# Linear attention into a two-layer MLP: the start of batch 0 reordered, batch 2 transposed by DMA, the last output tile in two column halves

## The chip, the cores and the metric

The kernel runs on one core of a Trainium2 chip. The metric is the device time of one execution in microseconds, over several runs of the same program; lower is better. Besides, one execution was recorded by the hardware profiler, and all rows below come from that one. Engines are named as in its page: PE multiplies matrices (PEld is its loading of the stationary operand), DVE and ACT are the vector and scalar engines, POOL is the general engine that here issues the loads, SP issues the stores and the other transfers.

## What is computed

```python
batch, n_heads, seq, head_dim = (8, 8, 576, 64)      # q, k, v, float32
n_tokens, d_model, d_ff = (4608, 512, 2048)          # w_in [512, 2048], w_out [2048, 512]

def phi(x):
    return np.where(x > 0, x, np.exp(x) - 1.0) + 1.0
q_p, k_p = (phi(q), phi(k))
kv = np.einsum('bhsd,bhse->bhde', k_p, v)
z = np.sum(k_p, axis=2)
num = np.einsum('bhsd,bhde->bhse', q_p, kv)
den = np.einsum('bhsd,bhd->bhs', q_p, z)[..., None] + 1e-06
attn = num / den
x = attn.transpose(0, 2, 1, 3).reshape(4608, 512)
h = x @ w_in
g = h - np.tanh(h)
out = g @ w_out
```

kv and z need k (kv needs v too), den needs q and z, and num needs q and kv. So 1/den can be had without v.

## The kernel before

**Tiling.** Attention goes by batch (eight of 576 tokens), the MLP by chunk (nine of 512 tokens). x is kept transposed in `xT`, 128 rows for each of four head pairs p. Layer 1 of a chunk is 16 tiles `fi` of 128 hidden columns, each of four matmuls with 512 moving columns over p (L270); ACT's tanh (L275) and DVE's subtraction (L276) turn each into a slice of `gT`. Layer 2 gives four output tiles `i` of 128 tokens, each of 16 matmuls with 512 columns (L285), then a copy by ACT (L290) and two stores by SP (L293).

**Attention of a batch.** `phi` (L120) is one exp on ACT, then two instructions on DVE, `r` and the product, for each half `i` of the heads; q and k each have two such halves. q is transposed into `qT`, either by PE with an identity matrix and copies from PSUM (`a_qT_pe`, L146: five tiles that ACT copies, four that DVE copies, for each half) or by one DMA of SP (`a_qT_dma`, L140). `kv_mm` (L161) makes kv with 18 matmuls for each half; a third block of ones behind v makes z in the same matmuls. `a_kv` or `a_kv_half` multiplies the result with a mask into `kz`. `a_den` (L185) makes den and its reciprocal `rden`. The reciprocal is then spread over the partitions: by two DMA steps through DRAM for batches from 2 on (`a_spread`, L205), by PE and a selection matrix `sel` for batches 0 and 1 (`a_spread_pe`, L252). num is made by `num_mm` (L217). For batches from 2 on DVE multiplies it with the spread reciprocal from PSUM straight into `xT` (`a_num`, L228); for batches 0 and 1 ACT first copies it to `ns` (L245) and DVE scales it later (`a_scale`, L262).

**Buffers.** PSUM is one tile of eight banks, handed out in a fixed order: in the chunks from 1 on, six for the MLP (`dense`) and two for attention (`attn`, banks 6 and 7). The raw k and q have one buffer each, v, `qT` and `kz` two.

**Order.** The order of the instructions on each engine is written out by hand and is the order of the program text; the framework adds only the waits. Before the loops, batch 0 goes through attention alone (L337 to L358): 36 matmuls on zeros keep PE busy, then come phi of k, phi of q, and the rest. POOL first issues the loads of k, q and v of batch 0, then makes the identity, then loads `w_in` (L300 to L305). In the loop over chunks, the work of attention of the next two batches is hung behind certain tiles: `s1[fi]` runs behind layer-1 tile `fi`, `s2[s]` behind a quarter (four matmuls) of an output tile of layer 2. Batch 1 runs in chunk 0, batch 2 from the end of chunk 0 into chunk 1. The only transposes by PE in the loops are those of batch 1 (chunk 0) and of batch 2 (chunk 1, L406, one part behind each of the tiles 4 to 7).

Of the kernel before, what the change touches and what calls it, by code (L numbers as in the profile page):

```python
# [18 lines left out]
def kernel(  # L19
# [74 lines left out]
    def load_k(b):  # L94
        load_kq(b, k, k_t, "kraw")

    def load_q(b):
        load_kq(b, q, q_t, "qraw")
# [32 lines left out]
    def a_kphi(b, i):  # L131
        phi(b, k_t, kp_t, "kp", i)

    def a_qphi(b, i):
        phi(b, q_t, qp_t, "qp", i)
# [10 lines left out]
    def a_qT_pe(b, i, banks, parts=(0, 1)):  # L146
        if i == 0 and 0 in parts:
            new_qT(b)
        for n in parts:
            j0, j1 = ((0, 5), (5, 9))[n]  # L150
            ps = banks().bitcast(BF16).rearrange("p (j t) -> p j t", t=128)
            for j in range(j0, j1):
                nc.tensor.transpose(ps[:, j - j0, :], qp_t[b][:, i, j].rearrange("p h d -> p (h d)"), ident)
            src = ps[:, 0:j1 - j0, :]
            dst = qT_t[b][:, i, j0:j1].rearrange("p j g t -> p j (g t)")
            if n == 0:
                nc.scalar.copy(dst, src)  # L157
            else:
                nc.vector.tensor_copy(dst, src)

    def kv_mm(b, i, ps):  # L161
        kp, vt = kp_t[b], v_b[b % 2]
        for j in range(J):
            for hg in range(2):
                r = slice(64 * hg, 64 * hg + 64)
                nc.tensor.matmul(ps[hg], kp[r, i, j].rearrange("p h d -> p (h d)"),  # L166
                                 vt[r, i, :, j, :], start=(j == 0), stop=(j == J - 1))
# [6 lines left out]
        for hg in range(2):  # L174
            nc.vector.tensor_mul(kz_t[b][:, hg], ps[hg][:, :, 0:160], mask[:, hg])  # L175

    def a_kv_half(b, i, banks):
        if i == 0:
            kz_t[b] = work.tile([128, 2, 2, 160], BF16, name="kz")
        ps = [banks()[:, 0:192] for hg in range(2)]  # L180
        kv_mm(b, i, ps)
        for hg in range(2):
            nc.vector.tensor_mul(kz_t[b][:, hg, i, :], ps[hg][:, 0:160], mask[:, hg, i, :])

    def a_den(b, banks):  # L185

# [58 lines left out]
    def a_num_copy(b, ns, p, banks):  # L245
        ps = num_mm(b, p, banks)
        if p < NP:
            nc.scalar.copy(ns[:, p, 0:8, :], ps)
        else:
            nc.scalar.copy(ns[:, :, 8, :], ps[:, 0:NP, :])  # L250

    def a_spread_pe(b, bank0, pairs):  # L252

        bp = ps_all[:, bank0:bank0 + 4, :]
        for n, p in enumerate(pairs):
            for t in range(4):
                r = slice(32 * t, 32 * t + 32)
                nc.tensor.matmul(bp[:, t, 144 * n:144 * n + 144], sel[r, p].rearrange("p h e -> p (h e)"),  # L258
                                 rden_t[b][r], start=True, stop=True)
        return bp  # L260

    def a_scale(b, p, ns, bp, o):  # L262
        nc.vector.tensor_mul(  # L263
            xT[:, p, S * b:S * b + S].rearrange("p (j t c) -> p t j c", j=J, t=4),
            ns[:, p].rearrange("p j (t c) -> p t j c", t=4),
            bp[:, :, o:o + 144].rearrange("p t (j c) -> p t j c", c=16))


    def l1mm(c, fi, h, p):
        nc.tensor.matmul(h, w_in_sb[:, p, fi * 128:(fi + 1) * 128], xT[:, p, c * 512:(c + 1) * 512],  # L270
                         start=(p == 0), stop=(p == NP - 1))

    def l1act(fi, h, gT):
        th = mpool.tile([128, 512], F32, name="th")
# [10 lines left out]
            nc.tensor.matmul(o, gT[:, fi, i * 128:(i + 1) * 128], w_out_sb[:, fi, :],  # L285
                             start=(fi == 0), stop=(fi == NF - 1))

    def evac(c, i, o):
        osb = opool.tile([128, DM], F32, name="osb")
        nc.scalar.copy(osb, o)  # L290
        for half in range(2):
            b, j = divmod(2 * (4 * c + i) + half, J)
            nc.sync.dma_start(out=out[b * S:(b + 1) * S, :].rearrange("(p j) m -> p j m", j=J)[:, j, :],  # L293
                              in_=osb[64 * half:64 * half + 64])


    nc.vector.memset(zero, 0.0)  # L297
    act0 = rpool.tile([128, 1], F32, name="act0")
    nc.scalar.activation(act0, zero[:, 0:1], AF.Exp)
    load_k(0)  # L300
    load_q(0)
    load_v(0)
    make_identity(nc, ident)
    for g in range(4):
# [29 lines left out]
        rest -= part  # L334


    for n in range(36):  # L337
        nc.tensor.matmul(ps_all[:, n % 4, :], zero[:, 0:128], zero, start=True, stop=True)  # L338
    for i in range(2):
        a_kphi(0, i)  # L340
    for i in range(2):
        a_qphi(0, i)
    side, kvb = Banks([4, 5, 6, 7]), Banks([0, 1, 2, 3])
    a_qT_pe(0, 0, side)
    a_kv_half(0, 0, kvb)
    a_qT_pe(0, 1, side)
    ns0 = new_ns(0)
    for p in (0, 2):
        a_num_copy(0, ns0, p, side)
    a_kv_half(0, 1, kvb)  # L350
    a_den(0, Banks([0]))
    a_num_copy(0, ns0, NP, Banks([1]))
    for p in (1, 3):
        a_num_copy(0, ns0, p, side)
    bp_a = a_spread_pe(0, 0, (0,))
    bp_b = a_spread_pe(0, 4, (1, 2, 3))
    for p in range(NP):
        a_scale(0, p, ns0, bp_b if p else bp_a, 144 * (p - 1) if p else 0)  # L358
    load_q(2)
    load_k(2)  # L360
    load_v(2)
# [1 line left out]
    for c in range(NC):  # L363
        gT = gpool.tile([128, NF, 512], BF16, name="gT")
        n1, n2 = c + 1, c + 2
        s1 = {i: [] for i in range(16)}
        s2 = {i: [] for i in range(16)}
        if c == 0:
            side = Banks([4, 5, 6, 7])
            sub = {}  # L370

            def spread1(h):
                sub["bp"] = a_spread_pe(1, 4, (2 * h, 2 * h + 1))
                for p in (2 * h, 2 * h + 1):
                    a_scale(1, p, sub["ns"], sub["bp"], 144 * (p % 2))

            s1[11].append(lambda: a_kphi(1, 0))
            s1[13].append(lambda: a_kphi(1, 1))
            s1[15].append(lambda: a_qphi(1, 0))
            s2[1].append(lambda: a_qphi(1, 1))  # L380
            s2[4].append(lambda: a_qT_pe(1, 0, side))
            s2[5].append(lambda: a_qT_pe(1, 1, side))
            s2[6].append(lambda: a_kv(1, side))
            s2[8].append(lambda: a_den(1, side))
            def num1():
                sub["ns"] = new_ns(1)
                for p in (NP, 0, 1, 2, 3):
                    a_num_copy(1, sub["ns"], p, side)
                load_v(3)

            s2[9].append(num1)
            s2[11].append(lambda: spread1(0))
            s2[13].append(lambda: spread1(1))
            s2[14].append(lambda: a_qphi(2, 0))
            s2[15].append(lambda: a_qphi(2, 1))
        elif n1 < B:
            s1[9 if c == 1 else 5].append(lambda: a_kv(n1, attn))
            s1[11 if c == 1 else 8].append(lambda: (a_den(n1, attn), a_spread(n1)))
            for p in range(NP + 1):
                s2[9 + p].append(lambda p=p: a_num(n1, p))  # L400
            if c + 3 < B:
                s1[10].append(lambda: load_v(c + 3))
        if c == 1:
            s1[1].append(lambda: a_kphi(2, 0))
            s1[3].append(lambda: (a_kphi(2, 1), load_k(3), load_q(3)))
            for n in range(4):  # L406
                s1[4 + n].append(lambda n=n: a_qT_pe(2, n // 2, attn, (n % 2,)))
        if c >= 1 and n2 < B:
            if c > 1:

                s1[0].append(lambda: (gate(gT, 0), load_k(n2), load_q(n2)))
            d = 4 if c == 1 else 2
            s2[d].append(lambda: a_kphi(n2, 0))
            s2[d + 2].append(lambda: a_kphi(n2, 1))
            s2[d + 4].append(lambda: a_qphi(n2, 0))
            s2[d + 6].append(lambda: (a_qphi(n2, 1), a_qT_dma(n2)))
        if c == 0:

            hs = [ps_all[:, fi, :] for fi in range(4)]
            first = Banks([4, 5, 6, 7, 0, 1, 2, 3])  # L420
            for p in range(NP):
                for fi in range(4):
                    l1mm(c, fi, hs[fi], p)
            for fi in range(4):
                l1act(fi, hs[fi], gT)
        for fi in range(4 if c == 0 else 0, NF):
            h = first() if c == 0 else dense()
            for p in range(NP):
                l1mm(c, fi, h, p)
            l1act(fi, h, gT)  # L430
            for f in s1[fi]:
                f()
        os_ = {}
        for s in range(16):

            (g, i) = divmod(s, 4) if c == 0 else (s % 4, s // 4)
            if g == 0:
                os_[i] = ps_all[:, i, :] if c == 0 else dense()
            l2mm(gT, os_[i], i, 4 * g, 4 * g + 4)
            if g == 3:  # L440
                evac(c, i, os_[i])
            for f in s2[s]:
                f()
# [30 lines left out]
```

## Time and profile before

| | |
|---|---|
| median of three runs | 302.88 us (302.36 to 304.21) |
| the profiled execution | 303.09 us |
| its span, first to last instruction | 301.3 us |
| mean granted PE clock | 0.998 of full |
| L270, layer 1 | 576 matmuls, 128.5 us |
| L285, layer 2 | 576 matmuls, 131.6 us |
| L166, kv | 288 matmuls, 13.7 us |
| DMA queues, share of 16 engines' span | loads by POOL 37.8%, those of SP 29.0% |

In the rows of the timeline the columns are: start in us from the start of the span; duration of the row; engine; line; operation; what is written and what is read; shape; count; and in brackets the idle time of the engine just before and what ended it. The busy time of a row with a count can hold idle time between its instructions. A stretch of the busy-time view shows, behind the length, each engine's busy us with its number of instructions, then the granted clock, the DMA share and GB/s.

Chunk 0 runs from 19.9 to 53.3 us in that execution, chunk 1 to 87.3, and the last matmul ends at 296.4. Each load of k or q of batch 0 is 144 KB, in four parts; the parts of one tensor are issued some 0.6 us apart.

### The profile page before, as it was taken

To read this page: it belongs to the slowest core of one execution; us is meant where nothing else is said; L and a number is where in the kernel's file an instruction comes from. 1 tells how busy PE (TensorE), PEld (TensorE's weight loads), DVE (VectorE), ACT (ScalarE), POOL (GpSimd) and SP (SyncE) were. 2 spreads that over 40 slices of the span, in tenths; PEclk is the share of its full clock that TensorE was granted. 3 is DMA by queue.
4 is the path that set the end of the run, shared out by engine and by line. 5 is a ranking of instruction groups with operands and counts; after the bars stand their busy time and mean duration, and the time that the engine had idled before them with its cause. 6 is when DMAs were issued, how large, how long until landed. Compare 5 with 4: busy or idle time off the path is not lost.

```text
span 301.3 us, 4706 instructions
## 1 busy us (share of the span) xinstructions
PE 291.9 (97%) x1790; PEld 138.3 (46%) x1790; DVE 180.2 (60%) x304; ACT 149.6 (50%) x230; POOL 52.1 (17%) x91
## 2 busy tenths in 40 slices
PE   8989999989999999999999999999999999999993
PEld 3454454444445444544454445444544444444441
DVE  7658944887557854785478557865681467008500
ACT  3638914954734653565256625662562166136420
POOL 8873263051006000600050003000000000000000
PEclk9999999999999999999999999999999999999999
DMA  6999999677969786967697778477108310130033
GB/s 90 189 207 206 205 207 205 181 120 135 212 111 177 122 200 138 155 116 190 140 151 135 179 148 128 87 173 148 38 4 193 71 35 0 37 86 18 2 70 70
DMA packets 36406, 38.23 MB, mean 127 GB/s; under 512 B 14432, under 2 KB 31008, under 8 KB 35616
## 3 DMA queue, kind: packets, MB, share of 16 engines
q0 software_dynamic: 17600, 18.35, 37.8%
q1 hardware_dynamic: 18784, 19.58, 29.0%
q8 instruction: 14, 0.23, 0.3%
q14 instruction: 8, 0.07, 0.1%
HBM read 43.78 MB, written 9.55 MB: 177 GB/s over the span
## 4 chain that ended last, share of the span: by engine, by line
PE 79%; DMA 9%; DVE 5%; ACT 2%; issue 1%; POOL 1%; SPq 0%; DVEq 0%; POOLq 0%; ACTq 0%
PE ps_all L270 38%; PE ps_all L285 33%; DMA qraw<-in_q_dram 4%; PE ps_all L166 4%; DMA out_dram<-osb 2%; DVE gT L276 2%; PE ps_all L221 2%; DMA v<-in_v_dram 2%; ACT e L127 1%; ACT osb L290 1%; DVE kp L129 1%; PE ps_all L191 1%; POOL kraw L85 1%; DVE r L128 1%; DVE qp L129 1%
## 5 line engine op out<-in xcount | busy, mean ns | idle before, releaser
L285 PE MATMUL ps_all<-w_out_sb,gT 128*128 128x512 bf16 x576 | 131.6, 379 | 0.0
L270 PE MATMUL ps_all<-xT,w_in_sb 128*128 128x512 bf16 x576 | 128.5, 379 | 0.2 <-DVE xT L263 0.2
L276 DVE TENSOR_TENSOR gT<-ps_all,th 128x512 bf16<-128x512 f32 x144 | 96.8, 687 | 53.0 <-ACT th L275 52.6
L275 ACT ACTIVATE th<-ps_all 128x512 f32<-128x512 f32 x144 | 85.3, 600 | 51.7 <-PE ps_all L270 47.2
L285 PEld LDWEIGHTS <-gT 128*128 128x128 bf16 x576 | 55.5, 98 | 65.7 <-issue 0.2
L270 PEld LDWEIGHTS <-w_in_sb 128*128 128x128 bf16 x576 | 55.2, 98 | 65.9 <-issue 1.1
L290 ACT COPY osb<-ps_all 128x512 f32<-128x512 f32 x36 | 21.1, 586 | 79.6 <-PE ps_all L285 59.5
L232 DVE TENSOR_TENSOR xT<-ps_all,rdb 128x512 bf16<-128x512 f32 x24 | 16.4, 689 | 11.8 <-PE ps_all L221 11.8
L104 POOL DMA_DIRECT2D v<-in_v_dram x32 | 19.2, 615 | 18.7 <-PE ps_all L166 5.7
L127 ACT ACTIVATE e<-kraw 128x1152 bf16<-128x1152 bf16 x16 | 18.5, 1165 | 5.1 <-DMA kraw<-in_k_dram 5.1
L129 DVE TENSOR_TENSOR kp<-e,r 128x1152 bf16<-128x1152 bf16 x16 | 12.1, 759 | 14.1 <-ACT e L127 13.0
L127 ACT ACTIVATE e<-qraw 128x1152 bf16<-128x1152 bf16 x16 | 18.4, 1166 | 0.9 <-DMA qraw<-in_q_dram 0.9
L129 DVE TENSOR_TENSOR qp<-e,r 128x1152 bf16<-128x1152 bf16 x16 | 12.1, 758 | 8.1 <-ACT e L127 7.3
L281 POOL COPY g<-gT 1x1 bf16<-1x1 bf16 x4 | 0.7, 176 | 92.9 <-DVE gT L276 92.9
L166 PE MATMUL ps_all<-v,kp 64*128 64x192 bf16 x288 | 13.7, 243 | 0.0
L166 PEld LDWEIGHTS <-kp 64*128 64x128 bf16 x288 | 11.5, 94 | 3.5 <-issue 2.9
L338 PE MATMUL ps_all<-zero 128*128 128x512 bf16 x36 | 10.4, 461 | 1.2 <-DVE zero L297 1.2
L221 PE MATMUL ps_all<-qT,kz 128*128 128x512 bf16 x32 | 11.3, 380 | 0.0
L89 POOL DMA_DIRECT2D kraw<-in_k_dram x14 | 8.7, 628 | 11.8 <-ACT qT L157 10.4
L89 POOL DMA_DIRECT2D qraw<-in_q_dram x14 | 8.7, 642 | 5.9 <-DVE r L128 5.9
L263 DVE TENSOR_TENSOR xT<-ns,ps_all 128x576 bf16<-128x576 f32 x8 | 5.6, 750 | 5.0 <-PE ps_all L258 5.0
L175 DVE TENSOR_TENSOR kz<-ps_all,mask 128x320 bf16<-128x320 f32 x14 | 6.2, 485 | 3.7 <-PE ps_all L166 3.7
(45 smaller groups left out, 92.8 us busy)
## 6 DMA issues: line engine op xcount, KB each, us to landing
out_dram<-osb SPq DMA_DIRECT2D x72, 128.0 KB
rdb<-ds SPq DMA_DIRECT2D x12, 576.0 KB
v<-in_v_dram POOLq DMA_DIRECT2D x32, 144.0 KB, 6.7
kraw<-in_k_dram POOLq DMA_DIRECT2D x14, 288.0 KB, 5.0
qraw<-in_q_dram POOLq DMA_DIRECT2D x14, 288.0 KB, 6.8
w_in_sb<-in_moe_w_in_dram POOLq DMA_DIRECT2D x4, 512.0 KB, 10.1
w_out_sb<-in_moe_w_out_dram POOLq DMA_DIRECT2D x4, 512.0 KB, 12.1
kraw<-in_k_dram POOLq DMA_DIRECT2D x4, 144.0 KB, 3.8
```

The lines of the kernel that those rows point to most:

```text
L89: nc.gpsimd.dma_start(out=t[64 * hg:64 * hg + 64].rearrange("p i h j d -> p (i h) (j d)"), in_=src[b, 4 * hg:4 * hg + 4].rearrange("h (p j ...
L104: nc.gpsimd.dma_start(out=v_b[b % 2][64 * hg:64 * hg + 64, i, 0:2].rearrange("p h j d -> p h (j d)"), in_=v[b, h0:h0 + 2].rearrange("h (p ...
L127: nc.scalar.activation(e, x, AF.Exp)
L129: nc.vector.tensor_tensor(store[b][:, i].rearrange("p j h d -> p h j d"), e, r, ALU.min)
L166: nc.tensor.matmul(ps[hg], kp[r, i, j].rearrange("p h d -> p (h d)"), vt[r, i, :, j, :], start=(j == 0), stop=(j == J - 1))
L221: nc.tensor.matmul(ps, kz[:, p // 2, p % 2, 0:128], qT[:, p % 2, 0:8, p // 2, :], start=True, stop=True)
L232: nc.vector.tensor_mul(xT[:, p, S * b:S * b + 512].rearrange("p (j t c) -> p j t c", j=8, t=4), ps.rearrange("p j (t c) -> p j t c", t=4), ...
L270: nc.tensor.matmul(h, w_in_sb[:, p, fi * 128:(fi + 1) * 128], xT[:, p, c * 512:(c + 1) * 512], start=(p == 0), stop=(p == NP - 1))
L275: nc.scalar.activation(th, h, AF.Tanh)
L276: nc.vector.tensor_sub(gT[:, fi, :], h, th)
L285: nc.tensor.matmul(o, gT[:, fi, i * 128:(i + 1) * 128], w_out_sb[:, fi, :], start=(fi == 0), stop=(fi == NF - 1))
L290: nc.scalar.copy(osb, o)
```

## The change

There are three parts.

**Batch 0.** q is loaded before k. The 36 matmuls on zeros are split into 22, 9 and 4 (one fewer), around the transposes of q, which now stand ahead of phi of k in the program. z is made by matmuls of its own, with 32 columns of ones, so that den and its reciprocal come before kv of the second half; kv has 128 moving columns in place of 192. num is made and copied by halves; the spread takes the pairs (0, 2) and then (1, 3), in place of (0) and then (1, 2, 3). The first four tiles of chunk 0 take p in the order 0, 2, 1, 3.

**Batch 2.** Its transposes by PE in chunk 1 are gone; SP issues a DMA transpose at the end of chunk 0. In chunk 1 kv moves from tile 9 to 7, den and the spread from 11 to 13, and the loads of k and q of batch 3 from tile 3 to a gate behind tile 10 (`gate` is a copy of one element of `gT` on POOL, which waits for that tile).

**The last output tile** of the last chunk is made in two halves of 256 columns in two PSUM banks, each with 16 matmuls, a copy and two stores of its own.

```diff
-    def a_kv_half(b, i, banks):
...
+    def b0_z(i):
         if i == 0:
-            kz_t[b] = work.tile([128, 2, 2, 160], BF16, name="kz")
-        ps = [banks()[:, 0:192] for hg in range(2)]
-        kv_mm(b, i, ps)
+            kz_t[0] = work.tile([128, 2, 2, 160], BF16, name="kz")
+        for j in range(J):
+            for hg in range(2):
+                r = slice(64 * hg, 64 * hg + 64)
+                nc.tensor.matmul(ps_all[:, 2 * i + hg, 0:32], kp_t[0][r, i, j].rearrange("p h d -> p (h d)"),
+                                 one[r, 0:32], start=(j == 0), stop=(j == J - 1))
+        nc.vector.tensor_mul(kz_t[0][:, :, i, 128:160], ps_all[:, 2 * i:2 * i + 2, 0:32], mask[:, :, i, 128:160])
+
+    def b0_kv(i):
+        for j in range(J):
+            for hg in range(2):
+                r = slice(64 * hg, 64 * hg + 64)
+                nc.tensor.matmul(ps_all[:, 4 + 2 * i + hg, 0:128], kp_t[0][r, i, j].rearrange("p h d -> p (h d)"),
+                                 v_b[0][r, i, 0:2, j, :], start=(j == 0), stop=(j == J - 1))
+
+    def b0_kz(i):
+        nc.vector.tensor_mul(kz_t[0][:, :, i, 0:128], ps_all[:, 4 + 2 * i:6 + 2 * i, 0:128], mask[:, :, i, 0:128])
+
+    def b0_num(i, ns, rem):
+        kz, qT = kz_t[0], qT_t[0]
         for hg in range(2):
-            nc.vector.tensor_mul(kz_t[b][:, hg, i, :], ps[hg][:, 0:160], mask[:, hg, i, :])
+            nc.tensor.matmul(ps_all[:, rem, 64 * hg:64 * hg + 64], kz[:, hg, i, 0:128], qT[:, i, 8, hg, :],
+                             start=True, stop=True)
+        for hg in range(2):
+            nc.tensor.matmul(ps_all[:, 4 + hg, :].rearrange("p (j t) -> p j t", j=8), kz[:, hg, i, 0:128],
+                             qT[:, i, 0:8, hg, :], start=True, stop=True)
+        nc.scalar.copy(ns[:, i::2, 8, :], ps_all[:, rem, 0:128].rearrange("p (a t) -> p a t", a=2))
+        nc.scalar.copy(ns[:, i::2, 0:8, :].rearrange("p a j t -> p a (j t)"), ps_all[:, 4:6, :])
...
-    def evac(c, i, o):
+    def evac(c, i, o, f0=0, f1=None):
+        f1 = DM if f1 is None else f1
         osb = opool.tile([128, DM], F32, name="osb")
-        nc.scalar.copy(osb, o)
+        nc.scalar.copy(osb[:, f0:f1], o[:, f0:f1])
...
+    load_q(0)
     load_k(0)
-    load_q(0)
     load_v(0)
...
-    for n in range(36):
-        nc.tensor.matmul(ps_all[:, n % 4, :], zero[:, 0:128], zero, start=True, stop=True)
+    def spin(n):
+        for _ in range(n):
+            nc.tensor.matmul(ps_all[:, 2, :], zero[:, 0:128], zero, start=True, stop=True)
+
+    side = Banks([4, 5, 6, 7])
+    for i in range(2):
+        a_qphi(0, i)
+    spin(22)
+    a_qT_pe(0, 0, side)
+    spin(9)
+    a_qT_pe(0, 1, side)
     for i in range(2):
         a_kphi(0, i)
-    for i in range(2):
-        a_qphi(0, i)
-    side, kvb = Banks([4, 5, 6, 7]), Banks([0, 1, 2, 3])
-    a_qT_pe(0, 0, side)
-    a_kv_half(0, 0, kvb)
-    a_qT_pe(0, 1, side)
+    spin(4)
+    b0_z(0)
+    b0_kv(0)
+    b0_kz(0)
+    b0_z(1)
+    a_den(0, Banks([0]))
     ns0 = new_ns(0)
-    for p in (0, 2):
-        a_num_copy(0, ns0, p, side)
-    a_kv_half(0, 1, kvb)
-    a_den(0, Banks([0]))
-    a_num_copy(0, ns0, NP, Banks([1]))
-    for p in (1, 3):
-        a_num_copy(0, ns0, p, side)
-    bp_a = a_spread_pe(0, 0, (0,))
-    bp_b = a_spread_pe(0, 4, (1, 2, 3))
-    for p in range(NP):
-        a_scale(0, p, ns0, bp_b if p else bp_a, 144 * (p - 1) if p else 0)
+    b0_num(0, ns0, 1)
+    b0_kv(1)
+    bp_a = a_spread_pe(0, 0, (0, 2))
+    b0_kz(1)
+    b0_num(1, ns0, 6)
+    bp_b = a_spread_pe(0, 4, (1, 3))
+    for n, p in enumerate((0, 2, 1, 3)):
+        a_scale(0, p, ns0, (bp_a, bp_b)[n // 2], 144 * (n % 2))
...
-            s2[15].append(lambda: a_qphi(2, 1))
+            s2[15].append(lambda: (a_qphi(2, 1), a_qT_dma(2)))
         elif n1 < B:
-            s1[9 if c == 1 else 5].append(lambda: a_kv(n1, attn))
-            s1[11 if c == 1 else 8].append(lambda: (a_den(n1, attn), a_spread(n1)))
+            s1[7 if c == 1 else 5].append(lambda: a_kv(n1, attn))
+            s1[13 if c == 1 else 8].append(lambda: (a_den(n1, attn), a_spread(n1)))
...
-            s1[3].append(lambda: (a_kphi(2, 1), load_k(3), load_q(3)))
-            for n in range(4):
-                s1[4 + n].append(lambda n=n: a_qT_pe(2, n // 2, attn, (n % 2,)))
+            s1[3].append(lambda: a_kphi(2, 1))
         if c >= 1 and n2 < B:
-            if c > 1:
-
-                s1[0].append(lambda: (gate(gT, 0), load_k(n2), load_q(n2)))
+
+            l = 10 if c == 1 else 0
+            s1[l].append(lambda: (gate(gT, l), load_k(n2), load_q(n2)))
...
-            for p in range(NP):
+            for n, p in enumerate((0, 2, 1, 3)):
                 for fi in range(4):
-                    l1mm(c, fi, hs[fi], p)
+                    l1mm(c, fi, hs[fi], p, n)
...
+            if c == NC - 1 and i == 3:
+
+                if g == 0:
+                    o2 = dense()
+                    for u, o in enumerate((os_[i], o2)):
+                        f = slice(256 * u, 256 * u + 256)
+                        for fi in range(NF):
+                            nc.tensor.matmul(o[:, f], gT[:, fi, 384:512], w_out_sb[:, fi, f],
+                                             start=(fi == 0), stop=(fi == NF - 1))
+                        evac(c, i, o, 256 * u, 256 * u + 256)
+                continue
```

## The prediction

> **What bounds the kernel now.** I read the page first, then busy time by stage, then the timeline of the first 20 us, of the second chunk and of the end. In the page, rows 1 and 2 say that PE is busy nearly always and at full clock; the chain says the same.
>
> ```profile
> PE 291.9 (97%) x1790; PEld 138.3 (46%) x1790; DVE 180.2 (60%) x304; ACT 149.6 (50%) x230; POOL 52.1 (17%) x91
> ...
> PE 79%; DMA 9%; DVE 5%; ACT 2%; issue 1%; POOL 1%; SPq 0%; DVEq 0%; POOLq 0%; ACTq 0%
> ```
>
> So time can come only from places where PE waits, or from work taken off PE. Busy time by stage (columns: stretch; its length; then PE, PEld, DVE, ACT, POOL) finds them:
>
> ```profile
> 19.89:53.28 33.39, 33.39 (x238) 16.48 (x238) 22.54 (x38) 18.58 (x31) 11.85 (x20) 1.00 1.22 206
> 53.28:72.33 19.05, 17.31 (x136) 8.77 (x134) 15.80 (x29) 13.90 (x22) 4.84 (x8) 1.00 0.82 159
> ...
> 87.28:103.27 15.99, 15.99 (x118) 7.79 (x116) 11.72 (x19) 9.54 (x16) 5.03 (x9) 1.00 0.95 162
> ...
> 282.60:301.30 18.70, 13.81 (x64) 6.05 (x62) 1.19 (x2) 2.94 (x5) 0.00 (x0) 0.96 0.25 57
> ```
>
> The reader is to see: chunk 0 (first row) has no gap, so a late start reaches the end undiminished. Layer 1 of chunk 1 (second row) takes 3.06 us more than that of chunk 2 (third row): 1.32 of transposes and 1.74 of idle PE. The last row has 4.9 us after the last matmul. The start, in the timeline:
>
> ```profile
> 9.60 0.29 POOL masks.py:199 TENSOR_SCALAR_AFFINE_SELECT ident<-ident 128x128 bf16<-128x128 bf16 x1
> ...
> 10.24 1.16 ACT L127 ACTIVATE e<-qraw 128x1152 bf16<-128x1152 bf16 x1 [0.57 <-DMA qraw<-in_q_dram]
> ...
> 11.73 1.16 ACT L127 ACTIVATE e<-qraw 128x1152 bf16<-128x1152 bf16 x1 [0.33 <-DMA qraw<-in_q_dram]
> ...
> 12.26 0.68 PE L153 MATMUL ps_all<-ident,qp 128*128 128x128 bf16 x9 [0.62 <-DVE qp L129]
> 12.80 0.68 ACT L157 COPY qT<-ps_all 128x640 bf16<-128x640 bf16 x1
> ...
> 13.22 0.76 DVE L129 TENSOR_TENSOR qp<-e,r 128x1152 bf16<-128x1152 bf16 x1
> ...
> 17.08 1.06 DVE L202 RECIPROCAL rden<-ps_all 128x144 f32<-128x144 f32 x1 [0.42 <-PE ps_all L195]
> ...
> 19.89 12.46 PE L270 MATMUL ps_all<-xT,w_in_sb 128*128 128x512 bf16 x57 [0.21 <-DVE xT L263]
> ```
>
> The exps follow the loads (starts 5.15, 8.51, 10.24, 11.73); the last phi ends at 13.98 and layer 1 starts 5.9 us later. By issue plus time to landing, v lands from 12.3 to 14.5. The identity exists only from 9.89, because POOL makes it after its v issues.
>
> **What the Trainium skill says.** TensorE: Matmul & The Clock Gate, section "Architectural detail: the array is 16× 32×32, not 1× 128×128", says that ScalarE and VectorE take their queues strictly in order and that only PE pulls weight loads ahead. No row here contradicts it; the forecast rests on it. Its section "What's actually happening" says that PE runs at half clock until one window of some 3.4 us was busy, and falls back after an idle window. The trace agrees on the first: spin matmuls start 0.43 us apart until 6.29 and 0.216 after; it shows no fall in the start. Its section "Back-to-back issue gap" gives N/2.4 + 2.5 ns: 216 for 512 columns, as here (64 in 13.81 us), 109 for 256, and warns that small N is slower; transposes of 128 columns take 75 here (9 in 0.68), not 56.
>
> **Part 1, the start.** q is loaded before k. The four landings keep their times, so q's exps start at 5.15 and 8.51, and qp ends at 7.26 and 10.5 (as kp does now). In program order follow 22 spins, the transposes of pair 0, 9 spins, those of pair 1, and only then phi of k. ACT and DVE therefore reach k's phi after the second transpose's copies. Step by step:
> - 22 spins: 12 cold in 5.1 us, 10 warm, end at 8.45. The transposes wait for the identity: 9.92 to 10.60.
> - 9 spins at 0.216: 1.94, to 12.54; second transposes 0.68, to 13.22. ACT's copy starts 0.54 after their start (12.26 to 12.80 above), 13.08 to 13.76.
> - exp of k: 13.8 to 14.95 and to 16.1, though k landed by 10.2 and 11.7. DVE's two products (0.76) with r between end at 15.75 and 17.0: **3.0 us after the present last phi**.
> - z of pair 1, 18 matmuls of 32 columns: no row shows these. Below: 25 ns each; above: 49 (L166 with 192 columns, 18 in 0.89). I take 37, the pace of L166's weight loads (18 in 0.67): 17.85 with the wake of DVE. Mask product, at most 0.27 (128x160): 18.2. den to reciprocal 0.59 as now: 18.8; reciprocal 1.06: 19.87.
> - v has landed since 14.5, before z of pair 0 can even start at 15.8: nothing is left to hide behind v.
> - kz of pair 1 is behind the reciprocal on DVE, 0.42 (L237's shape): 20.3. PE's first spread (16 half passes, 0.77 less the drain: 0.55) ends at 20.5; num of pair 1, two of 512 and two of 64 columns, reaches ACT by 21.15.
> - It reuses banks 4 to 6, and the second spread takes 4 to 7, so PE, in order, waits until ACT has copied num: 1024 columns, twice 0.54, 22.3. Spread 0.55 and layer 1 at 23.0; 23.1 with the rests. The four scales (0.7 each) start at 20.9 and hide there, two before and two under 1.73 us of matmuls.
>
> That is **+3.2 us** on 19.89. Below: if identity and spins cost nothing, phi of k ends at 13.98 and the same chain gives 20.0, +0. Above: the clock falls, +5. w_in's parts land from 17.0 to 25.1, and no part is needed sooner than now.
>
> **Part 2, chunk 1.** 18 transposes, their four copies (ACT 1.5, DVE 0.82) and PE's idle go:
>
> ```profile
> 60.98 0.44 PE L153 MATMUL ps_all<-ident,qp 128*128 128x128 bf16 x5 [0.99 <-ACT qT L157]
> ...
> 63.03 0.38 PE L153 MATMUL ps_all<-ident,qp 128*128 128x128 bf16 x4 [0.75 <-DVE qT L159]
> ...
> 68.50 0.43 PE L191 MATMUL ps_all<-qT,kz 128*32 128x144 bf16 x16
> ...
> 73.68 1.13 SPq L212 DMA_DIRECT2D rdb<-ds  x2
> ```
>
> - The gain is at most 3.06. What is late next is kp: kv moves from the ninth tile to the seventh, 60.2 on the present clock; kp's second half ends at 61.46, the first 18 matmuls of kv (0.8) hide most, 0.5 remains. Layer 1 takes 16.5 (ends 69.8): **-2.55**.
> - The DMA transpose is issued once qp ends (56.6), behind the eight stores that SP issues until 56.2. The one of batch 3 took SP 2.78 us from 84.45, its packets run until about 90: 5.6. So qT lands by some 62.5; den at tile 13 needs it at 67.7. Covered by 5 us. Behind it on SP wait only the den writes of 70.5.
> - den goes from tile 11 to 13, while the stage shrinks. DVE now ends rden at 71.22, 1.1 before layer 2; then at 70.45, 0.65 after its start. From rden to the last packet of rdb it is 9.6 us now (the DMA packet records end at 80.8): 80.05. num 0 comes at 78.4, num 1 at 79.5; num 2 at 80.6 needs a bank that the product of num 0 frees 0.8 after rdb. PE waits 0.25.
> - POOL's loads of k and q of batch 3 (four, 1.18 MB) move from 61.1 behind a gate on tile 10's gT, about 67.2, after v of batch 4. At 200 GB/s they need 5.9 us, until 74.6, beside the start of rdb, which now has the DMA engines alone: 0 to 1.5 more. In all a new wait of 0.25 to 1.7; I take 0.7. They land before k's phi at 74; behind the gate stands nothing on POOL before chunk 2.
>
> Net **-1.85**, from -2.9 (no waits) to -0.3 (kp and rdb both late by a us more).
>
> **Part 3, the end.** 16 matmuls of 512 become 32 of 256: +0.04 at 109 ns; above, 130 ns, +0.7. The last copy is 128x256, 0.37 (L250) for 0.59: -0.22. The last two stores carry half: their packets run 298.0 to 299.6 now; I take 0.2 of that, 0 to 0.3. **-0.35**, from -0.55 to +0.5. The first half's stores (1.2 us of SP) are issued 1.7 us earlier.
>
> **Sum.** +3.2 - 1.85 - 0.35 = +1.0 on the profiled execution's 303.09 (span 301.3, 1.8 around it), 304.1. The median of the runs is 302.88, 0.2 lower: 303.9.
>
> **Rivals.** A change of under 1%, 3.0 us, can't be told from none here.
> - *Start hidden.* Transposes come when data allow, spins fall into gaps: +0 to +1 for the start, total -1.2 to -2.2, 300.7 at the best, 299.5 with all of part 2. For it: 22 and 9 spins bridge 7.3 to 10.5 exactly if the identity were early. Against: 9.89 on POOL.
> - *Clock falls*, the slower side. PE idles at 8.45 to 9.9, 14.1 to 15.8 and 21.3 to 22.3, longer than now. If the clock falls in one window, spins or layer 1 run at 0.43 for some 3.4 us: +1.7 to 1.9, 305.6 to 306; two windows 307.5. It decides from 1.9 us of price. Against: no gap is a whole window.
> - *Not what it says.* qT by DMA lands after 67.7 and PE waits as long as it did for transposes: part 2 gives 0, 305.7. Against: 5 us of slack.
>
> **How the numbers follow.** My forecast 0.60 (302 to 305.8), start hidden 0.14 (half of it past 1%), clock or longer start 0.20, transpose late 0.06. Faster 0.07, same 0.71, slower 0.22. Leaving out about 1 in 10 on each side: 300.3 to 307.0.
>
> **What would show it.** Right: exp of k about 13.8 behind a copy of qT; layer 1 of chunk 0 at 23; no PE row for qT in chunk 1, whose layer 1 takes 16.5; products of batch 2 waiting for rdb; tail matmuls 0.109 apart. Wrong: k's exp at 10.2, layer 1 before 21, spins 0.43 apart after 9, or a wait at den for qT.

## The result and the profile after

The changed kernel takes 311.49 us, median of three runs (310.38 to 312.56), against 302.62 for the kernel before: ratio 1.0281, 95% interval 1.0218 to 1.0345. Here and below, a slow run, one that is over 1.5% above the fastest run of its kernel, is left out of the changed versions' times (of the changed kernel that is a fourth run, 315.25 us at a mean granted clock of 0.967 for 0.977 to 0.988). The change costs 8.9 us, where 303.9 us, some +1.0, was forecast, with 307.0 as the upper end. The profiled execution took 311.49 us, its span is 309.7.

Cut where the first matmul of each stage starts (in the last row 0.16 us behind it, in both), the two profiled executions differ so:

| stage | before, us | after, us | difference | forecast |
|---|---|---|---|---|
| to the first matmul of layer 1 | 19.89 | 24.65 | +4.76 | +3.2 |
| chunk 0 | 33.39 | 33.40 | 0 | 0 |
| chunk 1, layer 1 | 19.05 | 16.47 | -2.58 | -2.55 |
| chunk 1, layer 2 | 14.79 | 21.72 | +6.93 | +0.7 |
| chunk 2 to layer 1 of chunk 8 | 195.48 | 195.47 | 0 | 0 |
| layer 2 of chunk 8 to the end | 18.70 | 17.99 | -0.71 | -0.35 |

The sum is +8.4, the difference of the spans. (Chunk 2 of the kernel before starts at 87.12, not at 87.28, where the text above cuts.) Four rows came out about as forecast. The fourth row is most of the loss, and the first one is 1.6 us worse than its forecast.

From the page of the changed kernel, two rows of the 40 slices (each digit a busy share, or a granted clock, in tenths; a slice is 7.7 us):

```profile
PE   8589999999939999999999999999999999999994
...
PEclk9959999999989999999999999999999999999999
```

Two places stand out: the second and third slices, and the twelfth. In each PE first waits, and then its clock falls. The trace's clock record has half speed from 15.7 to 22.5 us and from 90.8 to 94.2. In the profile of before the clock never falls between the first warm-up and the last matmul.

The same in busy time by stage (length; then PE, PEld, DVE, ACT, POOL; then granted clock, DMA share, GB/s):

```profile
24.65:58.05 33.40, 32.92 (x237) 16.51 (x239) 21.99 (x37) 18.49 (x31) 10.43 (x17) 1.00 1.11 187
58.05:74.52 16.47, 16.00 (x116) 7.74 (x116) 14.47 (x26) 12.81 (x20) 4.99 (x9) 1.00 0.73 128
74.52:96.24 21.72, 16.37 (x72) 7.20 (x72) 9.37 (x16) 6.58 (x8) 0.00 (x0) 0.92 0.75 155
...
291.71:309.70 17.99, 13.81 (x80) 7.63 (x78) 1.19 (x2) 3.10 (x6) 0.00 (x0) 0.99 0.25 58
```

In the third row PE has 5.35 us of idle time, and its busy 16.37 are 1.6 more than in the kernel before, which is busy for all of its 14.79, with the same matmuls: that is the half clock.

**Where layer 2 of chunk 1 waits.** Its timeline (start, length, engine, line, operation, count, and in brackets the idle time before and what ended it):

```profile
71.80 1.23 POOL L89 DMA_DIRECT2D kraw<-in_k_dram  x2 [0.31 <-issue]
...
73.02 1.24 POOL L89 DMA_DIRECT2D qraw<-in_q_dram  x2
...
75.17 1.36 SPq L236 DMA_DIRECT2D ds<-rden  x4
...
81.37 1.13 SPq L239 DMA_DIRECT2D rdb<-ds  x2
...
89.81 1.29 DVE L259 TENSOR_TENSOR xT<-ps_all,rdb 128x512 bf16<-128x512 f32 x2 [5.74 <-DMA rdb<-ds]
90.55 0.38 PE L248 MATMUL ps_all<-qT,kz 128*128 128x512 bf16 x1 [5.08 <-DVE xT L259]
```

The writes of the kernel before, whose next step, at 73.68, is shown above:

```profile
71.25 1.34 SPq L209 DMA_DIRECT2D ds<-rden  x4
```

The reciprocal is spread in two steps: four writes of 4.5 KB to DRAM (`ds`), then two reads that copy them to all partitions (`rdb`). SP may issue the second step only when the first has landed. It waited 4.7 us for that; in the kernel before it was 0.9 (the writes' issue ends at 72.59, the second step starts at 73.68). The packet records show what lay in between: the packets of the loads of k and q of batch 3 (1152 bytes each) run from 73 to 80.5, and those of the four writes (576 bytes) come only from 79.2 to 80.5. Then the copies to all partitions take their 8 us, the product of batch 2 starts only at 89.8, both attention banks are full, and PE stands for 5.08 us.

**The start.** The timeline of the changed kernel:

```profile
9.05 0.29 POOL masks.py:199 TENSOR_SCALAR_AFFINE_SELECT ident<-ident 128x128 bf16<-128x128 bf16 x1
...
9.39 0.66 PE L153 MATMUL ps_all<-ident,qp 128*128 128x128 bf16 x9 [1.17 <-POOL ident masks.py:199]
...
9.89 2.10 PE L367 MATMUL ps_all<-zero 128*128 128x512 bf16 x9
...
12.31 0.69 ACT L157 COPY qT<-ps_all 128x640 bf16<-128x640 bf16 x1 [1.75 <-PE ps_all L153]
...
12.90 2.22 ACT L127 ACTIVATE e<-kraw 128x1152 bf16<-128x1152 bf16 x2
...
14.10 1.08 DVE L129 TENSOR_TENSOR kp<-e,r 128x1152 bf16<-128x1152 bf16 x1 [0.77 <-ACT e L127]
15.11 0.92 DVE L128 TENSOR_SCALAR r<-kraw 128x1152 bf16<-128x1152 bf16 x1
...
15.24 0.39 PE L185 MATMUL ps_all<-one,kp 64*128 64x32 bf16 x18 [1.88 <-DVE kp L129]
...
16.13 1.02 DVE L129 TENSOR_TENSOR kp<-e,r 128x1152 bf16<-128x1152 bf16 x1
...
18.55 1.06 DVE L229 RECIPROCAL rden<-ps_all 128x144 f32<-128x144 f32 x1 [0.66 <-PE ps_all L222]
...
23.94 0.77 PE L285 MATMUL ps_all<-rden,sel 32*128 32x144 f32 x16 [1.10 <-ACT ns L210]
...
24.65 13.99 PE L297 MATMUL ps_all<-xT,w_in_sb 128*128 128x512 bf16 x62
```

The order of events is the forecast one: the transposes wait for the identity, ACT's second copy for nine spins (matmuls on zeros), the exps of k for that copy. The two exps then run back to back, so k had landed before. PE idles 1.88 us before z, the clock falls at 15.7, and what PE does from there to 22.5 is done at half speed.

**The end.** The last tile in the changed kernel:

```profile
301.91 3.66 PE L478 MATMUL ps_all<-w_out_sb,gT 128*128 128x256 bf16 x32
...
303.86 0.37 ACT L318 COPY osb<-ps_all 128x256 f32<-128x256 f32 x1 [1.16 <-PE ps_all L478]
305.61 0.37 ACT L318 COPY osb<-ps_all 128x256 f32<-128x256 f32 x1 [1.38 <-PE ps_all L478]
```

The 32 matmuls start 0.109 us apart. From the first of them to the start of the last copy it is 3.70 us, 0.05 more than for the 16 of before (292.80 to 296.45).

### The profile page after: what moved, and what is told of

Read it like the earlier page. It is cut to its first block, busy times and chain, and to the rows that moved or that the text cites. A ratio compares the mean times of both kernels' runs of the same rounds, so it can differ in the third digit from the quotient of the medians.

```text
span 309.7 us, 4746 instructions
## 1 busy us (share of the span) xinstructions
PE 292.0 (94%) x1794; PEld 140.1 (45%) x1823; DVE 180.4 (58%) x302; ACT 148.7 (48%) x228; POOL 52.7 (17%) x92
## 4 chain that ended last, share of the span: by engine, by line
PE 84%; DMA 6%; DVE 3%; issue 2%; ACT 2%; POOL 1%; SPq 0%; DVEq 0%; ACTq 0%; POOLq 0%
PE ps_all L297 37%; PE ps_all L312 36%; PE ps_all L166 3%; DMA rdb<-ds 3%; PE ps_all L248 2%; DMA ds<-rden 2%; DMA qraw<-in_q_dram 2%; PE ps_all L478 1%; PE ps_all L285 1%; ACT e L127 1%; PE ps_all L218 1%; DVE gT L303 1%; DVE kp L129 1%; PE ps_all L153 1%; PE ps_all L367 1%
## 5 line engine op out<-in xcount | busy, mean ns | idle before, releaser
L312 PE MATMUL ps_all<-w_out_sb,gT 128*128 128x512 bf16 x547 | 127.5, 382 | 1.1 <-issue 0.5
L297 PE MATMUL ps_all<-xT,w_in_sb 128*128 128x512 bf16 x561 | 126.9, 379 | 0.9 <-issue 0.2
L312 PEld LDWEIGHTS <-gT 128*128 128x128 bf16 x560 | 54.3, 98 | 70.0 <-issue 7.2
L318 ACT COPY osb<-ps_all 128x512 f32<-128x512 f32 (+1 forms) x37 | 21.2, 574 | 86.3 <-PE ps_all L312 63.2
L248 PE MATMUL ps_all<-qT,kz 128*128 128x512 bf16 x28 | 10.4, 388 | 5.1 <-DVE xT L259 5.1
L166 PE MATMUL ps_all<-v,kp 64*128 64x192 bf16 x252 | 11.8, 243 | 0.3 <-DVE kp L129 0.3
L166 PEld LDWEIGHTS <-kp 64*128 64x128 bf16 x252 | 10.0, 94 | 3.5 <-issue 2.5
L128 DVE TENSOR_SCALAR r<-kraw 128x1152 bf16<-128x1152 bf16 x16 | 7.7, 481 | 1.4 <-DMA kraw<-in_k_dram 1.4
```

What stands on the lines that cost most here:

```text
L248: nc.tensor.matmul(ps, kz[:, p // 2, p % 2, 0:128], qT[:, p % 2, 0:8, p // 2, :], start=True, stop=True)
L318: nc.scalar.copy(osb[:, f0:f1], o[:, f0:f1])
```

## The experiments

What was expected of each version, ahead of its result, is quoted first. Times are medians; ratios are to the kernel before, run on the same chip, whose median was 302.8 to 302.9 in each set.

### The three parts, each alone

Part 1 alone is the changed kernel with these lines back as they were (and without the gate in chunk 1, and the last tile whole). The other two were made in the same way, with the old start.

```diff
# part 1 alone, against the changed kernel
-            s2[15].append(lambda: (a_qphi(2, 1), a_qT_dma(2)))
+            s2[15].append(lambda: a_qphi(2, 1))
-            s1[7 if c == 1 else 5].append(lambda: a_kv(n1, attn))
-            s1[13 if c == 1 else 8].append(lambda: (a_den(n1, attn), a_spread(n1)))
+            s1[9 if c == 1 else 5].append(lambda: a_kv(n1, attn))
+            s1[11 if c == 1 else 8].append(lambda: (a_den(n1, attn), a_spread(n1)))
-            s1[3].append(lambda: a_kphi(2, 1))
+            s1[3].append(lambda: (a_kphi(2, 1), load_k(3), load_q(3)))
+            for n in range(4):
+                s1[4 + n].append(lambda n=n: a_qT_pe(2, n // 2, attn, (n % 2,)))
```

> The kernel before with part 1 alone (q first, z and den ahead of kv, spins split). Theory: part 1 costs 4.8 us in the trace of the changed kernel (layer 1 starts at 24.65 for 19.89) and nothing gives it back, so +4.8 on 302.6, about 307.4; layer 1 at 23.2 to 25, depending on whether the clock falls. Rival, that the two parts only add up badly together (a late start shifts the loads against batch 2): under +3.

Measured: 307.57 (306.83 to 308.70), ratio 1.0165 (1.0112 to 1.0218), some +5. The run that kept the full clock (a mean of 1.000) took 306.83, so the start costs some 4 us without any fall of the clock. The rival falls.

> The kernel before with part 2 alone (DMA transpose, kv at tile 7, den at 13, loads of batch 3 behind tile 10). Theory: layer 1 of chunk 1 16.5 for 19.05, layer 2 21.7 for 14.95 as in the changed kernel, so +4.2, about 306.8. Rival, that the wait in layer 2 comes from the late start of part 1: layer 2 near 15, total 302.6 - 2.5 = 300.1.

Measured: 306.66 (306.44 to 307.05), ratio 1.0132 (1.0100 to 1.0164). Layer 1 of chunk 1 is 16.47, layer 2 21.22, with this PE wait:

```profile
85.17 0.58 PE L256 MATMUL ps_all<-qT,kz 128*128 128x512 bf16 x1 [4.85 <-DVE xT L267]
```

So the wait does not need the late start; it belongs to part 2.

> The kernel before with part 3 alone. Theory: 0.7 less behind the last matmul and 0.06 more before it, as in the changed kernel: about 302.0. Rival, nothing gained: 302.6.

Measured: 301.91, ratio 0.9969 (0.9958 to 0.9979): the end gains 0.9 us.

### What makes the spread late

One of the two late moves undone in each of the next two runs, in the changed kernel.

```diff
# loads of k and q of batch 3 back at tile 3
-            s1[3].append(lambda: a_kphi(2, 1))
+            s1[3].append(lambda: (a_kphi(2, 1), load_k(3), load_q(3)))
-            l = 10 if c == 1 else 0
-            s1[l].append(lambda: (gate(gT, l), load_k(n2), load_q(n2)))
+            if c > 1:
+                s1[0].append(lambda: (gate(gT, 0), load_k(n2), load_q(n2)))
```

> The changed kernel with the loads of k and q of batch 3 back at tile 3, without the gate; den stays at tile 13. Theory (the den writes to DRAM queue behind 1.2 MB of loads on the DMA engines): the writes land within 2 us of their issue, for 5 now, the product of batch 2 no longer waits more than 1 us, layer 2 of chunk 1 falls from 21.7 to about 15.5, total about 305.5. Rival (den two tiles later is enough to make the spread late): layer 2 stays above 18, total above 308.5.

Measured: 307.65, ratio 1.0156 (1.009 to 1.0222), 3.8 us less than the changed kernel.

```profile
87.62 0.38 PE L248 MATMUL ps_all<-qT,kz 128*128 128x512 bf16 x1 [2.00 <-DVE xT L259]
```

SP waits 1.5 us for the writes, as the theory says, but PE still waits 2.00, the clock falls there for 3.4 us, and layer 2 is 18.64, above 18 as the rival says, while the total lies between the two. So the loads cost 3 us of the wait, not all of it; the next run asks whether den at tile 13 holds the rest.

```diff
# den and the spread of batch 2 back at tile 11
-            s1[13 if c == 1 else 8].append(lambda: (a_den(n1, attn), a_spread(n1)))
+            s1[11 if c == 1 else 8].append(lambda: (a_den(n1, attn), a_spread(n1)))
```

> The changed kernel with den of batch 2 back at tile 11, the loads of batch 3 still behind tile 10. Theory (the den writes stand behind the loads on the DMA engines): rden is ready 1.8 us sooner, near 73, but the loads are issued from 71.8 and their packets run until 80.5, so the writes still land 4 us or more after their issue unless they slip in ahead of the first packets at 73; PE waits 3 us or more for the spread, layer 2 of chunk 1 at 19 or more, total 309 to 311. Rival (den too late): the wait goes, layer 2 below 17, total near 306.

Measured: 308.18, ratio 1.0177 (1.0152 to 1.0201).

```profile
88.91 0.38 PE L248 MATMUL ps_all<-qT,kz 128*128 128x512 bf16 x1 [3.40 <-DVE xT L259]
```

SP still waits 4.5 us for the writes and PE 3.40: issuing them 1.7 us sooner lets the spread start 1.6 sooner and changes next to nothing in SP's wait. So den at tile 13 holds 1.7 us of PE's wait. Layer 2 is 18.6, with no fall of the clock, which is why the total lies below the stated range. The rival falls.

> The changed kernel with both undone: loads of k and q of batch 3 at tile 3 and den at tile 11. The run with the loads alone undone still waited 2.0 us for a product of batch 2. Theory (two causes that add: the loads ahead of the writes, 3 us, and den 1.8 us later): no wait above 0.5 us, layer 2 of chunk 1 at 15.0 to 15.6, no fall of the clock there, total 304.5 to 305.5 (start +4 to +5.6, chunk 1 -2.5, end -0.9). Rival (v of batch 4, now right behind k and q, takes the place of the gated loads): the writes land 3 us after issue, layer 2 above 16.5, total above 306.5.

Measured: 306.25, ratio 1.013 (1.0089 to 1.0171). The rival is the better one here (only its total, above 306.5, is just missed): SP waits 3.5 us for the writes, PE 2.06, and layer 2 takes 17.3. The kernel before has the same three loads (k and q of batch 3, v of batch 4) in front of the writes, and their packets make one row there too, from 62.4 to 73.4 us. But its writes were issued from 71.25 to 72.59, when that row was about to end; here they are issued from 72.58 to 73.96 and the row runs on to 76.8, since layer 1 has become shorter.

The same with the old start and part 3, that is, a version meant to beat both kernels (called best_b below):

> The kernel before with part 3 and part 2 without its two late moves: DMA transpose, kv at tile 7, but loads of batch 3 at tile 3 and den at tile 11; the start is that of the kernel before. Theory: layer 1 of chunk 1 16.5 for 19.05, layer 2 15.0 to 15.5, end 0.9 less: 302.6 - 2.5 - 0.9 + 0.3 = 299.5. Rival (the spread still waits behind v of batch 4): above 301.

Measured: 302.05, ratio 0.9984 (0.9969 to 1.0). The rival again. The timeline of this kernel:

```profile
68.22 1.39 SPq L244 DMA_DIRECT2D ds<-rden  x4
73.19 1.13 SPq L247 DMA_DIRECT2D rdb<-ds  x2
...
82.40 0.38 PE L256 MATMUL ps_all<-qT,kz 128*128 128x512 bf16 x1 [2.15 <-DVE xT L267]
```

The writes are issued 7 us sooner than in the changed kernel (and 3.0 sooner than before), but stand in a row of 1.8 MB of loads whose packets run from 62.0 to 72.6; theirs run from 71.5 to 72.1. If the theory of the next run holds, it is enough to take v of batch 4, which is needed only in chunk 3, out of that row:

```diff
# against best_b, the kernel above
+    def gate_x():
+        g0 = rpool.tile([1, 1], BF16, name="g0")
+        nc.gpsimd.tensor_copy(g0, xT[0:1, 0, 2 * S:2 * S + 1])
-            if c + 3 < B:
+            if c > 1 and c + 3 < B:
                 s1[10].append(lambda: load_v(c + 3))
         if c == 1:
+            s2[9].append(lambda: (gate_x(), load_v(4)))
```

> As best_b, but the load of v of batch 4 is issued only behind the first product of batch 2 in chunk 1 (a one-element copy on POOL from xT waits for it), so that only k and q of batch 3 stand ahead of the den writes. Theory (any load issued ahead of the writes delays them, whatever tensor it is): the 1.2 MB of k and q end near 68.5, the writes of 68.2 land within 2 us, the spread is complete by 78 and PE does not wait for it; layer 2 of chunk 1 15.0 for 17.4, total 299.6 to 300.2, no fall of the clock. Rival (the spread itself, two copies of 0.6 MB, is what takes the time): PE still waits 1.5 us or more, total above 301.5.

Measured: 299.41 (299.1 to 300.03), ratio 0.9885 (0.9864 to 0.9906). Timeline and busy time of this kernel:

```profile
68.19 1.40 SPq L244 DMA_DIRECT2D ds<-rden  x4
70.89 1.13 SPq L247 DMA_DIRECT2D rdb<-ds  x2
...
80.05 0.38 PE L256 MATMUL ps_all<-qT,kz 128*128 128x512 bf16 x1
```

```profile
52.68:69.15 16.47, 16.16 (x118) 7.74 (x116) 14.81 (x26) 12.89 (x21) 2.46 (x4) 1.00 0.97 186
69.15:84.10 14.95, 14.95 (x75) 6.83 (x73) 8.82 (x16) 6.63 (x9) 2.57 (x5) 1.00 0.67 140
```

The writes are issued at the same instant as in the run before it and SP now waits 1.1 us for them, for 3.4; the spread starts 2.3 us sooner, PE waits for nothing, and layer 2, from its first matmul at 69.26 to that of chunk 2 at 84.05, is back at 14.79. The copies to all partitions are no faster than in the run before (7.1 and 7.5 us from issue to the last packet), so the rival falls. One load, moved to where nobody waits, is worth 2.6 us. The theory holds. What isn't shown is by which rule the packets of the writes are kept behind those of the loads; only that they are.

### What makes the start late

Spins instead of a gap before z, part 1 alone otherwise:

```diff
-    spin(4)
+    spin(12)
```

> The kernel before with part 1 and 12 spins for 4 ahead of z, which fill PE's gap there and change nothing that it waits for. Theory (part of the cost of the start is the clock, which falls when PE idles 1.9 us before z): full clock until layer 1 in most runs, layer 1 at 23.3 to 24, total 306 to 307, runs closer together than those of part 1 alone (306.8 to 311.8). Rival (the clock falls for the later gaps, behind the reciprocal and before the second spread): falls as often, 308 again.

Measured: 306.11 (305.61 to 306.62), ratio 1.010 (1.0074 to 1.0126), with clock means of 0.997 to 0.999. The timeline:

```profile
12.76 2.75 PE L367 MATMUL ps_all<-zero 128*128 128x512 bf16 x12
...
13.33 2.22 ACT L127 ACTIVATE e<-kraw 128x1152 bf16<-128x1152 bf16 x2
...
15.66 0.39 PE L185 MATMUL ps_all<-one,kp 64*128 64x32 bf16 x18 [0.15 <-DVE kp L129]
...
22.56 0.77 PE L285 MATMUL ps_all<-rden,sel 32*128 32x144 f32 x16 [1.10 <-ACT ns L210]
23.27 2.98 PE L297 MATMUL ps_all<-xT,w_in_sb 128*128 128x512 bf16 x13
```

The gap before z is gone and so is the fall of the clock; layer 1 starts at 23.27, 1.4 sooner than in the changed kernel, although q landed later here and the exps of k start 0.43 later. From these exps to layer 1 it is 9.94 us, against 11.75 in the changed kernel: the fall of the clock cost 1.8 us. What is left, 3.4 us on 19.89, is not the clock. (In the other four profiles with the old start, layer 1 begins between 18.92 and 19.48, so half a us of such a difference can be the loads.)

```diff
# start_joined: part 1 alone, but
     spin(22)
     a_qT_pe(0, 0, side)
-    spin(9)
     a_qT_pe(0, 1, side)
...
-    spin(4)
+    spin(13)
# start_ident: start_joined, but
-    load_v(0)
     make_identity(nc, ident)
+    load_v(0)
```

> The kernel before with part 1, but without spins between the two transposes: 22 spins, both transposes, phi of k, then 13 spins. Theory (9 spins hold back ACT's second copy and so k's exps by their 1.7 us, and PE then idles at z, which lets the clock fall): exps of k from 11.3, second z at about 15.5, layer 1 at 22 to 22.5, full clock in most runs, total 304.8 to 305.5. Rival (the start is slow through the chain of halves behind z alone): layer 1 not more than 0.5 sooner than in the run of part 1 alone, total above 306.5.

Measured: 304.76 (303.83 to 305.75), ratio 1.006 (1.0034 to 1.0085), 2.8 us less than part 1 alone. The nine spins in the way, together with the gap they leave later, are thus the larger part of the loss. In the profiled run the exps of k start at 12.04, since q's second half landed up to 1.1 us later than in the other profiles, and the clock fell there all the same, at 11.8, after a wait of 2.41 for the identity; layer 1 starts at 22.57.

> As start_joined (part 1, both transposes together, 13 spins behind them), and POOL makes the identity before it issues the loads of v, 2.5 us sooner. Theory (PE waits for the identity, and through the copies so do k's exps): the first transposes at 8.0 to 8.5 for 10.35, exps of k within 1 us of their landing (10.2, 11.7), layer 1 at 20.5 to 21.5, total 303.2 to 304.2. Rival (the rest of the cost lies in the chain behind z, num by halves and two spreads in turn): layer 1 not before 22, total above 304.5.

Measured: 305.54, ratio 1.0086 (1.0063 to 1.0109), no better than the run before it. The first transposes do start at 7.68, but the second ones wait for q (10.52), exps of k start at 11.60, the clock falls again at 11.6, and the 13 spins, now slow, hold PE: z starts at 15.62 and could have started 2 us before (the first half of phi of k was ready at 13.56). So this run doesn't tell the identity's share from the rest: it traded one wait for another. Layer 1 starts at 22.13 and the total is above 304.5, which is the rival's side. What the rest of the start's loss consists of, some 2 us with the transposes together, stays open.

### All together

The changed kernel with the three cures of chunk 1 and the filled gap:

> The changed kernel with all three parts and the cures of chunk 1 (loads of k and q of batch 3 at tile 3, v of batch 4 behind the first product of batch 2, den at tile 11) and 12 spins for 4 ahead of z. Theory (the parts add): start +3.3 as in the run with filled spins, chunk 1 -2.5, end -0.9: 302.8 to 303. Rival (the late start shifts the loads so that chunk 1 gains less): above 304.

Measured: 302.79, ratio 1.0006 (0.9991 to 1.0022). The parts add: the cures and the filled gap take 8.7 us off the changed kernel, and what is left of the start's loss eats the whole gain of chunk 1 and of the end.

## Why the prediction was wrong, step by step

**Wrong: the new wait in chunk 1.** The step read "from rden to the last packet of rdb it is 9.6 us now" and then, for the moved loads, "beside the start of rdb ... 0 to 1.5 more. In all a new wait of 0.25 to 1.7; I take 0.7". Measured: 5.35 us of idle PE, 5.08 of them that one wait, and 1.6 of half clock behind it, 6.93 in all. The step priced the loads as bandwidth taken from the big copies of `rdb`. What they delayed were the four tiny writes ahead of it: 4.7 us of waiting for 18 KB. Of the two dependent transfers, the first paid for the row of packets in front of it. The forecast had both times needed to see it, the loads until 74.6 and the writes at 70.5, and kept the 9.6 us, measured where the loads were about to end, for a place where they were just beginning. den at tile 13 for 11 made it worse by about 1.7 us (5.08 against 3.40 of PE wait).

**Wrong in size: the start.** +3.2 was forecast, +4.76 measured, 1.55 us more, and three terms make it up. Up to the exps of k the steps came in the forecast order but 0.9 us sooner (12.90 for 13.8), 0.5 of it because q's second half landed before the time assumed for it (exp at 7.97 for 8.51), and with it came the identity (first transposes at 9.39 for 9.92): that is luck. From there to layer 1 the forecast has 9.3 us, and with the gap filled it was 9.94. DVE's phi of k took 4.2 us from the first exp to its end where the forecast has 3.2 (its products took 1.08 and 1.02 for 0.76, the second `r` 0.92 for 0.45), and the rest was 0.4 shorter: z's 18 matmuls took 0.39 to the end of the last, for 0.67, and less than the lower bound of 0.45, since they came in pairs 3 ns apart with 25 ns from pair to pair. So 23.27 with the filled gap against the forecast 23.1 is in part two errors that cancel.

The remaining 1.8 us are the clock, which stood as a rival at 0.20, dismissed with "no gap is a whole window". The Trainium skill's page TensorE: Matmul & The Clock Gate, section "What's actually happening", has the clock fall after an idle window of some 3.4 us; here it fell after an idle time of 1.88 us, in a stretch of 3.41 us (12.31 to 15.73) of which PE was busy for 1.49, so the measurement decides. Its length, 6.8 and 3.4 us, does go by such windows.

**Right: layer 1 of chunk 1.** 16.47 against 16.5: the transposes' 1.32 and most of the idle time are gone, and kv waits 0.3 for phi of k (0.5 forecast). The DMA transpose was indeed covered: SP issued it at 61.45, its packets ended by 65.7, and den used it at 72.4. **Right in sign: the end**, 0.71 of gain in the profile and 0.9 in the runs of part 3 alone, against 0.35. The half-size copy gave its 0.22 and the extra matmuls cost 0.05; the rest, 0.54, came behind the last copy (4.26 us to the end before, 3.72 after), where the stores are, and of it only 0.2 was counted. **Right: chunk 0 passes a late start on undiminished** (33.39 and 33.40).

Of the rivals, "start hidden" and "not what it says" are out; "clock falls" is in, in two places, and the second is a consequence of the wait for the spread.

## What to carry to other kernels

When a load is moved, look first at which small transfers will then be issued behind it, above all those that another transfer waits for; in these runs it was their place in the row that set their time. Waiting spins stand in PE's order like any other instruction: put ahead of something that a second engine waits for, they delayed both here. And where PE gets a new gap of about 2 us, price the half clock behind it as well as the gap.

## What the runs showed of the hardware that was not expected

- Four writes of 4.5 KB, issued from SP, had SP wait for their landing for a time that goes with how long the packets of the loads from POOL in front of them still ran after the last write was issued: 0.9 to 1.5 us where these ended within 0.8 us (the kernel before; the loads of k and q back at tile 3; v of batch 4 moved), 3.4 and 3.5 where after some 3 (best_b; both late moves undone), 4.7 where after 3.9 (the changed kernel). The volume in front does not tell: it was 1.8 MB in four of these six, with 0.9, 1.5, 3.4 and 3.5 us. With den at tile 11, where part of the loads was issued behind the first writes, the wait was 4.5 us and the loads' packets ran on for 5.5.
- The length of a gap alone doesn't tell whether the clock falls: it fell after PE waits of 1.88 us (the start) and 2.00 (layer 2 with the loads early), and not after one of 3.40 (den at tile 11). What sorts them is how busy PE was within one stretch of 3.41 us. In each profile the recorded changes of the clock lie whole multiples of 3.41 us apart (to the rounding). Cut all 14 profiles into stretches at these times: each of the ten falls ahead of the last matmul follows a stretch in which PE was busy for 1.49 us or less, and of the other stretches at full clock that end ahead of the last matmul only one has as little (1.49, in the changed kernel, just before the stretch of its second fall); the rest have 1.54 or more. The wait of 3.40 was shared by two stretches with 1.54 and 1.82 us of busy PE. This was read from the traces, not tried by a run of its own. In best_b the same program ran with clock means of 0.998 to 1.000 in 301.26 to 302.14 us and of 0.994 in 302.96 to 303.93.
- DVE's product of phi, 0.76 us elsewhere, took 1.02 to 1.08 in the changed start, and the second `r` 0.92 for 0.45, while POOL filled `sel` (12.9 to 16.5 us). That was not tried by itself.
